# A decode step with a cached attention and a gated layer: w_q loaded first in eight loads of 16 rows, a shorter last stretch, and four tiny loads that nothing reads

## The chip, the cores and the metric

The kernel runs on one core of one Trainium2 chip. Its time is the device time of one execution in microseconds (us). Engines are named as in the profile: PE (TensorE matmul), PEld (its weight loads), DVE (VectorE), ACT (ScalarE), POOL (GpSimd), SP (SyncE, which here only issues loads). A core has 16 DMA engines, which all loads share.

## The reference

One token of 576 numbers goes through a layer norm and then through two branches, whose results are added to the token.

```python
xn  = layernorm(x)                                   # 1 x 576
q   = (xn @ wq) in 32 heads of 128                   # wq: 576 x 4096
k,v = last 4096 rows of the caches, 16 heads, each used by 2 query heads
o   = softmax(q k^T / sqrt(128)) v                   # 32 x 128
a   = o.reshape(4096) @ wo                           # wo: 4096 x 576
z   = gelu(xn @ w_in)                                # w_in: 576 x 4608
b   = (z[:2304] * (w_sp * layernorm(z[2304:]) + b_sp)) @ w_out   # w_out: 2304 x 576
out = x + a + b
```

Everything is bfloat16. Each number of the weights and of the used part of the caches is needed once: w_q 4.72 MB, keys and values 16.78 MB each, w_in 5.31 MB, w_o 4.72 MB and w_out 2.65 MB, 50.96 MB together.

## The kernel before, in words

**Loads.** SP issues all large loads, in the order of the program (L102 to L124): the first quarter of the keys `k0` in two halves, `wq` in two column pieces, `k1`, `v0`, `k2`, `v1`, `k3`, w_in (`win` and a rest `win8`), `v2`, `v3`, w_o (two pieces and a rest `wo28`) and w_out in four pieces: rows 0 to 11, 12 to 15, 16 and 17 of the 18 rows that each partition holds. Each of these loads writes all 128 partitions. The keys and values come in four quarters of four heads, 4.19 MB each.

**Buffers.** Two pools, `small` and `large`, hold two tiles each. A load into a pool's third tile has to wait until the first has been read by its last reader; so `k2` waits for the transposes of `k0`, `v1` for the matmuls with `wq`, and so on. SP issues in order, so a load that waits holds back all that follow.

**Completion counters.** The framework also gives every load, from ACT's three tiny ones on (`x_row` and two of `ws2`), one of eight completion counters in turn. A load first waits until the load that had its counter before has landed. A load that writes over part of what another load writes waits for that one too.

**Compute.** For each quarter b, `turn(b)` (L211) turns the keys with eight DVE transposes, `scores(b)` (L253) multiplies them with the query on PE, with a softmax on DVE and ACT, and `values(b)` (L289) multiplies with the values. The order is written out by hand at L357 to L368, with `turn(0)` at L219 ahead of the query's own work (L222 to L247). Each engine works in this order.

**The end.** `acc` (L378 to L391) sums, in four partition groups, 32 rows of w_o and the first `LATE` = 12 rows of w_out. The two halves of `acc` go to SBUF (`acc_sb`, L392 to L394), `fin` is cleared (L396), and `late` (L398) adds the remaining rows of w_out into `fin`, four matmuls a row. Just ahead of the last row it adds `acc_sb` (L405). `res` copies the result out of `fin` (L409), and SP stores it (L410).

Of the kernel before, what the change touches and what calls it, by code (L numbers as in the profile page):

```python
# [8 lines left out]
FP32 = mybir.dt.float32  # L9
BF16 = mybir.dt.bfloat16  # L10
# [4 lines left out]
P = 128  # L15
D = 576
# [12 lines left out]
NR = 9  # L29
# [3 lines left out]
FR = FH // P  # L33
# [3 lines left out]
ZW = P + ZPAD  # L37
SMALL = NU * DH
LARGE = WR * D
LATE = 12  # L40
OW = D // 4


# [1 line left out]
def kernel(  # L45
# [14 lines left out]
    nc = tc.nc  # L60
    ctx.enter_context(tc.manual_schedule())

    const = ctx.enter_context(tc.tile_pool(name="const", bufs=1))
# [8 lines left out]
    ps_v = ctx.enter_context(tc.tile_pool(name="ps_v", bufs=1, space=PS))  # L72
# [11 lines left out]
    def unit(name, width):  # L84
        pool = small if width == SMALL else large
        return pool.tile([P, width], BF16, name=name, tag="u")

    def halves(a):
        return a.rearrange("k (s c) -> (k s) c", s=2).rearrange("(p r) c -> p (r c)", r=NR)

    def load(t, view, width, cuts):
        for a, e in zip(cuts, cuts[1:]):
            nc.sync.dma_start(t[:, (a - cuts[0]) * width:(e - cuts[0]) * width], view[:, a * width:e * width])

    def load_kv(cache, name, b, width, cuts=(0, NU)):
        t = unit(f"{name}{b}", width)
        src = cache[0, HB * b:HB * (b + 1), SK - W:SK, :].rearrange("s (j u) d -> j s (u d)", u=NU)
        for a, e in zip(cuts, cuts[1:]):
            nc.sync.dma_start(t[:, a * DH:e * DH], src[:, :, a * DH:e * DH])  # L99
        return t  # L100

    kn, vn = {}, {}  # L102
    wq_v, win_v = halves(A_wq), halves(B_w_in)
    wo_v = A_wo.rearrange("(p r) n -> p (r n)", r=WR)
    kn[0] = load_kv(A_k_cache, "k", 0, SMALL, (0, NU // 2, NU))
    wq_t = unit("wq", LARGE)
    load(wq_t, wq_v, 2048, (0, 5, NR))
    kn[1] = load_kv(A_k_cache, "k", 1, SMALL)
    vn[0] = load_kv(A_v_cache, "v", 0, LARGE)
    kn[2] = load_kv(A_k_cache, "k", 2, SMALL)  # L110
    vn[1] = load_kv(A_v_cache, "v", 1, LARGE)
# [9 lines left out]
    wo28 = one.tile([P, FH], BF16, name="wo28", tag="side")  # L121
    load(wo28, wo_v, D, (28, WR))
    wout_t = unit("wout", LARGE)
    load(wout_t, B_w_out.rearrange("(p r) n -> p (r n)", r=FR), D, (0, LATE, 16, 17, FR))  # L124


    ident = const.tile([P, P], BF16, name="ident")
# [83 lines left out]
    def turn(b):  # L211
        for k in range(NK):
            t = ktp.tile([P, 2, 512, 2], BF16, name=f"kt{b}_{k}", tag="kt")
            nc.vector.transpose(  # L214
                t[:].rearrange("p c n e -> p (c n e)").bitcast(FP32),
                kn[b][:, UK * DH * k:UK * DH * (k + 1)].bitcast(FP32).rearrange("p (u c i) -> p c u i", c=2, i=32))
            kt[b, k] = t

    turn(0)  # L219


    q_ps = ps_s.tile([P, 512], FP32, name="q_ps", tag="s")  # L222
# [30 lines left out]
    def scores(b):  # L253
        sm = one.tile([P, 2, 512], FP32, name=f"sm{b}", tag="sm")
        mx = work.tile([P, 2], FP32, name=f"mx{b}", tag="mx")
        for kk in range(2):
            s_ps = ps_s.tile([P, 512], FP32, name=f"s{b}_{kk}", tag="s")
            for k4 in range(4):
                for ce in range(4):
                    c, e = divmod(ce, 2)  # L260
                    nc.tensor.matmul(s_ps[:], lhsT=zq[:, b, ce, ZPAD - 8 * k4:ZPAD - 8 * k4 + P],  # L261
                                     rhs=kt[b, 4 * kk + k4][:, c, :, e],
                                     start=k4 == 0 and ce == 0, stop=k4 == 3 and ce == 3)
            nc.vector.tensor_tensor_reduce(  # L264
                out=sm[:, kk, :].rearrange("p (n s) -> p n s", s=HB),
                in0=s_ps[:].rearrange("p (n s) -> p n s", s=HB),
                in1=cm[:].unsqueeze(1).to_broadcast([P, P, HB]), scale=SCALE, scalar=-3e38,
                op0=ALU.add, op1=ALU.max, accum_out=mx[:, kk:kk + 1])
        m1 = work.tile([P, 1], FP32, name=f"m1{b}", tag="m1")
        nc.vector.tensor_max(m1[:], mx[:, 0:1], mx[:, 1:2])  # L270
        tr = ps_m.tile([P, P], FP32, name=f"tr{b}", tag="m")
        nc.tensor.matmul(tr[:], lhsT=m1[:].to_broadcast([P, P]), rhs=ident_f[:], start=True, stop=True)  # L272
        m8 = work.tile([P, 8], FP32, name=f"m8{b}", tag="m8")
        nc.vector.tensor_reduce(out=m8[:], in_=tr[:].rearrange("p (a x) -> p x a", x=8), axis=AXX, op=ALU.max)
        mj = work.tile([P, 8], FP32, name=f"mj{b}", tag="mj")
        nm = work.tile([P, 1], FP32, name=f"nm{b}", tag="nm")
        nc.vector.tensor_tensor_reduce(out=mj[:], in0=m8[:], in1=sel8[:], scale=-1.0, scalar=0.0,  # L277
                                       op0=ALU.mult, op1=ALU.add, accum_out=nm[:])
        p = one.tile([P, 1024], BF16, name=f"p{b}", tag="p")
        l = work.tile([P, 1], FP32, name=f"l{b}", tag="l")  # L280
        nc.scalar.activation(p[:], sm[:].rearrange("p k n -> p (k n)"), ACT.Exp, bias=nm[:], accum_out=l[:])  # L281
        p_t[b] = work.tile([P, 2, 16, 32], BF16, name=f"pt{b}", tag="pt")
        nc.vector.transpose(p_t[b][:].rearrange("p k u m -> p (k u m)"), p[:])  # L283
        su = ps_m.tile([P, 8], FP32, name=f"su{b}", tag="m")
        nc.tensor.matmul(su[:], lhsT=l[:].to_broadcast([P, P]), rhs=sel8[:], start=True, stop=True)  # L285
        rms[b] = work.tile([P, 8], FP32, name=f"rm{b}", tag="rm")
        nc.vector.reciprocal(rms[b][:], su[:])
# [39 lines left out]
    def gate(z):  # L327
# [26 lines left out]
                                op0=ALU.mult, op1=ALU.add)  # L354
        nc.vector.tensor_mul(hv[:], G[:, 0, :], gz[:])

    scores(0)  # L357
    turn(1)
    scores(1)
# [15 lines left out]
    o_p = const.tile([P, WR], BF16, name="o_p")  # L375
    nc.vector.tensor_copy(o_p[:], op_ps[:])

    acc = [ps_a.tile([P, HW], FP32, name=f"acc{i}", tag="a") for i in range(2)]  # L378
    for i in range(2):
        nc.vector.memset(acc[i][:], 0.0)  # L380
# [4 lines left out]
    rows += [(o_p[:, r:r + 1], wo28[:, D * (r - 28):D * (r - 27)]) for r in range(28, WR)]  # L385
    rows += [(hv[:, r:r + 1], wout_t[:, D * r:D * (r + 1)]) for r in range(LATE)]
    for n in range(0, len(rows), 4):
# [4 lines left out]
    acc_sb = const.tile([P, D], FP32, name="acc_sb")  # L392
    nc.scalar.copy(acc_sb[:, 0:HW], acc[0][:])
    nc.vector.tensor_copy(acc_sb[:, HW:D], acc[1][:])  # L394
    fin = ps_v.tile([P, OW], FP32, name="fin", tag="pv")
    nc.vector.memset(fin[:], 0.0)  # L396

    def late(col, w, n, start=False, stop=False):  # L398
        for g in range(4):
            nc.tensor.matmul(fin[32 * g:32 * g + 1, :], lhsT=col, rhs=w[:, n + OW * g:n + OW * (g + 1)],  # L400
                             start=start, stop=stop, tile_position=(0, 32 * g))

    for r in range(LATE, FR):
        if r == FR - 1:
            late(selu[:, 0:1], acc_sb, 0)  # L405
        late(hv[:, r:r + 1], wout_t, D * r, start=r == LATE, stop=r == FR - 1)

# [33 lines left out]
```

## Time and profile before

| | |
|---|---|
| median of 2 runs | 128.5 us (128.49 to 128.52) |
| the profiled execution | 129.87 us, of which the span from the first to the last instruction is 128.1 us |
| mean granted PE clock | 0.867 |
| busy: PE, DVE, ACT, POOL | 57%, 51%, 8%, 3% of the span |
| DMA | 50.96 MB read, 398 GB/s over the span; SP's queue 93.4% of 16 engines' time |

The span is the profile's time axis, and every position below is counted from its start. The 1.77 us by which the profiled execution is longer than its span lie outside the instructions. The profiled execution was 1.37 us slower than the median of the runs, so a difference is worked out inside the profile and then put on the median.

### The profile page before, as it was taken

Reading aid. Unit: us, or ns where it says so; the run is one execution under the profiler, and the core shown is the slowest. Engines: PE = TensorE matmul, PEld = TensorE weight load, DVE = VectorE, ACT = ScalarE, POOL = GpSimd, SP = SyncE. Lnnn points to the kernel's source line nnn. Section 1 sums busy time; section 2 is a strip of 40 time slices with the busy share of each in tenths; the row PEclk is TensorE's granted clock in tenths of the full one; section 3 lists DMA queues with packets and bytes.
Section 4 is the critical chain, followed back from the end, with each engine's and each line's share of the span. In section 5 each row is a group of like instructions: output and inputs, shape, how many; then the busy total and the mean of one; then the engine's idle time right before and its main releaser. Section 6 shows DMA issues by size and latency. Waiting matters only on the chain.

```text
span 128.1 us, 1363 instructions
## 1 busy us (share of the span) xinstructions
PE 72.9 (57%) x554; PEld 33.7 (26%) x554; DVE 65.3 (51%) x133; ACT 10.2 (8%) x19; POOL 3.9 (3%) x10
## 2 busy tenths in 40 slices
PE   3200007349982399557599554899192389467070
PEld 3100002113421134123234233233080225323040
DVE  6689960060213999640899542998347620300010
ACT  3010000000003000031000031000300030100010
POOL 8400000000000000000000000000000000000000
PEclk9999999999999779986959999589977769855559
DMA  3999999998998999999989998999899899999810
GB/s 82 409 420 444 460 405 414 476 491 348 471 471 368 463 425 389 491 399 420 481 379 450 449 449 368 394 484 460 379 471 435 379 416 438 418 414 436 345 45 0
DMA packets 2899, 51.03 MB, mean 398 GB/s; under 512 B 333, under 2 KB 590, under 8 KB 974
## 3 DMA queue, kind: packets, MB, share of 16 engines
q1 hardware_dynamic: 2888, 50.96, 93.4%
q8 instruction: 4, 0.07, 0.2%
q14 instruction: 1, 0.01, 0.0%
q10 hardware_dynamic: 6, 0.00, 0.0%
HBM read 50.96 MB, written 0.00 MB: 398 GB/s over the span
## 4 chain that ended last, share of the span: by engine, by line
PE 37%; DMA 36%; DVE 16%; ACT 5%; SPq 2%; issue 1%; ACTq 0%
PE s L261 22%; DMA wout<-in_B_w_out_dram 19%; DMA wq<-in_A_wq_dram 17%; DVE kt L214 9%; PE pv L295 4%; ACT p L281 4%; PE z L319 3%; DVE sm L264 2%; PE op L303 2%; PE tr L272 2%; PE q_ps L225 2%; PE acc L390 1%; PE fin L400 1%; DVE pt L283 1%; SPq L99 1%
## 5 line engine op out<-in xcount | busy, mean ns | idle before, releaser
L261 PE MATMUL s<-kt,zq 128*128 128x512 bf16 x128 | 36.4, 448 | 5.3 <-DVE kt L214 4.9
L214 DVE STREAM_TRANSPOSE kt<-k 128x1024 f32<-128x1024 f32 x32 | 36.4, 1205 | 0.0
L261 PEld LDWEIGHTS <-zq 128*128 128x128 bf16 x128 | 14.0, 110 | 26.5 <-issue 15.3
L225 PE MATMUL q_ps<-wq,xw 128*32 128x512 bf16 x36 | 4.2, 626 | 16.4 <-DMA wq<-in_A_wq_dram 16.4
L264 DVE CUSTOM_DVE_ANT_1 sm<-s,cm 128x512 f32<-128x512 f32 x8 | 5.4, 677 | 10.1 <-PE s L261 10.1
L281 ACT ACTIVATE p<-sm,nm 128x1024 bf16<-128x1024 f32 x4 | 4.6, 1147 | 73.9 <-DVE nm L277 73.9
L295 PE MATMUL pv<-v,pt 128*32 128x512 bf16 x128 | 10.2, 477 | 0.0
L283 DVE STREAM_TRANSPOSE pt<-p 128x1024 bf16<-128x1024 bf16 x4 | 5.0, 1245 | 5.4 <-ACT p L281 5.4
L306 DVE TENSOR_TENSOR o_t<-op,rm 128x8 bf16<-128x8 f32 x4 | 0.7, 167 | 13.0 <-PE op L303 13.0
L225 PEld LDWEIGHTS <-xw 128*32 128x32 bf16 x36 | 1.4, 131 | 18.4 <-issue 18.4
L394 DVE COPY acc_sb<-acc 128x288 f32<-128x288 f32 x1 | 0.5, 458 | 11.2 <-PE acc L390 11.2
L285 PE MATMUL su<-sel,l 128*128 128x8 f32 x8 | 1.6, 266 | 7.6 <-ACT p L281 7.6
L303 PE MATMUL op<-selu,pvs 128*128 128x8 f32 x32 | 4.2, 259 | 2.8 <-ACT pvs L300 2.8
L390 PE MATMUL acc<-wo,o_p 128*1 128x288 bf16 x64 | 4.4, 439 | 1.7 <-DMA wo<-in_A_wo_dram 1.7
L303 PEld LDWEIGHTS op<-selu,pvs 128*128 128x128 f32 x32 | 3.9, 191 | 5.1 <-ACT pvs L300 5.1
L229 DVE CAST q_sb<-q_ps 128x512 bf16<-128x512 f32 x1 | 0.7, 692 | 8.2 <-PE q_ps L225 8.2
L295 PEld LDWEIGHTS <-pt 128*32 128x32 bf16 x128 | 3.6, 114 | 4.3 <-issue 2.6
L272 PE MATMUL tr<-ident_f,m 128*128 128x128 f32 x8 | 2.0, 326 | 3.9 <-DVE m L270 3.9
L319 PE MATMUL z<-win,xw 128*32 128x288 bf16 x72 | 3.6, 376 | 0.0
L285 PEld LDWEIGHTS su<-sel,l 128*128 128x128 f32 x8 | 1.2, 187 | 8.4 <-ACT p L281 8.4
L390 PE MATMUL acc<-wout,hv 128*1 128x288 bf16 x24 | 1.6, 438 | 3.0 <-DMA wout<-in_B_w_out_dram 3.0
L300 ACT COPY pvs<-pv 128x512 f32<-128x512 f32 x4 | 2.3, 586 | 11.0 <-PE pv L295 11.0
(95 smaller groups left out, 43.4 us busy)
## 6 DMA issues: line engine op xcount, KB each, us to landing
v<-in_A_v_cache_dram SPq DMA_DIRECT2D x4, 4096.0 KB, 25.8
k<-in_A_k_cache_dram SPq DMA_DIRECT2D x3, 4096.0 KB, 36.7
win<-in_B_w_in_dram SPq DMA_DIRECT2D x1, 4608.0 KB, 25.7
k<-in_A_k_cache_dram SPq DMA_DIRECT2D x2, 2048.0 KB, 9.8
wo<-in_A_wo_dram SPq DMA_DIRECT2D x2, 2016.0 KB, 27.1
wq<-in_A_wq_dram SPq DMA_DIRECT2D x1, 2560.0 KB, 17.4
wq<-in_A_wq_dram SPq DMA_DIRECT2D x1, 2048.0 KB, 21.6
wout<-in_B_w_out_dram SPq DMA_DIRECT2D x1, 1728.0 KB
```

What stands on the lines that cost most here:

```text
L214: nc.vector.transpose(t[:].rearrange("p c n e -> p (c n e)").bitcast(FP32), kn[b][:, UK * DH * k:UK * DH * (k + 1)].bitcast(FP32).rearrang ...
L225: nc.tensor.matmul(q_ps[32 * g:32 * g + 32, :], lhsT=xw[:, r, :], rhs=wq_t[:, 2048 * r + 512 * g:2048 * r + 512 * (g + 1)], start=r == 0, ...
L261: nc.tensor.matmul(s_ps[:], lhsT=zq[:, b, ce, ZPAD - 8 * k4:ZPAD - 8 * k4 + P], rhs=kt[b, 4 * kk + k4][:, c, :, e], start=k4 == 0 and ce = ...
L264: nc.vector.tensor_tensor_reduce(out=sm[:, kk, :].rearrange("p (n s) -> p n s", s=HB), in0=s_ps[:].rearrange("p (n s) -> p n s", s=HB), in ...
L272: nc.tensor.matmul(tr[:], lhsT=m1[:].to_broadcast([P, P]), rhs=ident_f[:], start=True, stop=True)
L281: nc.scalar.activation(p[:], sm[:].rearrange("p k n -> p (k n)"), ACT.Exp, bias=nm[:], accum_out=l[:])
L283: nc.vector.transpose(p_t[b][:].rearrange("p k u m -> p (k u m)"), p[:])
L285: nc.tensor.matmul(su[:], lhsT=l[:].to_broadcast([P, P]), rhs=sel8[:], start=True, stop=True)
L295: nc.tensor.matmul(pv[32 * g:32 * g + 32, :].rearrange("p (n d) -> p n d", n=4), lhsT=p_t[b][:, kk, u, :], rhs=v4[:, kk, u, :, :], start=k ...
L303: nc.tensor.matmul(op[:], lhsT=pvs[:, DH * u:DH * (u + 1)], rhs=selu[:, 8 * u:8 * u + 8], start=u == 0, stop=u == 3)
L319: nc.tensor.matmul(zp[i][32 * g:32 * g + 32, :], lhsT=xw[:, r, :], rhs=rhs, start=r == 0, stop=r == NR - 1, tile_position=(0, 32 * g))
L390: nc.tensor.matmul(acc[i][32 * g:32 * g + 1, :], lhsT=col, rhs=w[:, HW * i:HW * (i + 1)], start=n == 0 and g > 0, stop=n + 4 >= len(rows), ...
```

## The change

There are five edits.

- `wq` is loaded ahead of `k0`, in eight loads of 16 rows in place of two loads of 128 rows. Load e writes the partitions e, e+8, e+16, ... e+120, each with its whole row of 36,864 bytes.
- Behind `k1` come four loads into a new tile `few`: 8, 4, 2 and 1 rows of 64, 80, 96 and 112 bytes. They are cut from w_o, and nothing reads `few`. All four write its first row, so they overlap.
- `turn(0)` moves from ahead of the query's work to the line before `scores(0)`.
- `LATE` goes from 12 to 8, and w_out comes in five pieces: rows 0 to 7, 8 to 12, 13 to 15, 16 and 17.
- `fin` is made and cleared ahead of `acc`, and `acc_sb` is added ahead of row 13 instead of row 17.

```diff
-LATE = 12
+LATE = 8
...
+    wq_t = unit("wq", LARGE)
+    for e in range(8):
+        nc.sync.dma_start(wq_t[e::8, :], wq_v.rearrange("(i e) f -> e i f", e=8)[e])
     kn[0] = load_kv(A_k_cache, "k", 0, SMALL, (0, NU // 2, NU))
-    wq_t = unit("wq", LARGE)
-    load(wq_t, wq_v, 2048, (0, 5, NR))
     kn[1] = load_kv(A_k_cache, "k", 1, SMALL)
+    few = const.tile([16, 64], BF16, name="few")
+    for n, k in enumerate((8, 4, 2, 1)):
+        nc.sync.dma_start(few[0:k, 0:32 + 8 * n], A_wo[0:k, 0:32 + 8 * n])
     vn[0] = load_kv(A_v_cache, "v", 0, LARGE)
...
-    load(wout_t, B_w_out.rearrange("(p r) n -> p (r n)", r=FR), D, (0, LATE, 16, 17, FR))
+    load(wout_t, B_w_out.rearrange("(p r) n -> p (r n)", r=FR), D, (0, LATE, 13, 16, 17, FR))
...
-
-    turn(0)
...
+    turn(0)
     scores(0)
...
+    fin = ps_v.tile([P, OW], FP32, name="fin", tag="pv")
+    nc.vector.memset(fin[:], 0.0)
     acc = [ps_a.tile([P, HW], FP32, name=f"acc{i}", tag="a") for i in range(2)]
...
-    fin = ps_v.tile([P, OW], FP32, name="fin", tag="pv")
-    nc.vector.memset(fin[:], 0.0)
...
     for r in range(LATE, FR):
-        if r == FR - 1:
+        if r == 13:
             late(selu[:, 0:1], acc_sb, 0)
         late(hv[:, r:r + 1], wout_t, D * r, start=r == LATE, stop=r == FR - 1)
```

## The prediction

> **What bounds the kernel now.** I read the page's DMA row, then busy time by stage, then the chain that ended last, then SP's own timeline. The page's DMA row (40 slices, tenths of 16 engines) and one stage of 120 us:
>
> ```profile
> DMA  3999999998998999999989998999899899999810
> 2.00:122.00 120.00, 70.48 (x510) 32.48 (x514) 63.39 (x127) 9.80 (x18) 2.53 (x3) 0.87 1.00 424
> ```
>
> From 2 to 122 us the DMA engines are busy all the time (share 1.00), at 424 GB/s, while PE works 70 and DVE 63 of the 120 us. So the kernel is one stream of 50.96 MB; what matters is when it starts, whether it pauses, and what comes after its last byte. The chain, from the issue of w_out on:
>
> ```profile
> 97.30 24.18 DMA wout<-in_B_w_out_dram
> ...
> 121.52 1.64 PE acc L390 x24
> ...
> 123.19 0.46 DVE acc_sb L394
> ...
> 123.67 0.19 DVE fin L396
> ...
> 123.90 1.33 PE fin L400 x26
> ...
> 125.26 0.31 DVE res L409
> ```
>
> W_out is issued at 97.3 and waits 24 us behind other loads: the compute is far ahead of the stream. Behind it stand 3.7 us of work, and the store. SP's timeline (start, length of the issue):
>
> ```profile
> 0.74 1.29 SPq L99 DMA_DIRECT2D k<-in_A_k_cache_dram  x2
> 2.06 1.20 SPq L93 DMA_DIRECT2D wq<-in_A_wq_dram  x2
> 3.30 0.54 SPq L99 DMA_DIRECT2D k<-in_A_k_cache_dram  x1
> 3.89 0.60 SPq L99 DMA_DIRECT2D v<-in_A_v_cache_dram  x1
> 18.17 0.53 SPq L99 DMA_DIRECT2D k<-in_A_k_cache_dram  x1
> ```
>
> `v0` is issued at 3.9, while in the trace's DMA packet records its first packet starts at 33.1, when `k1`'s last ones end (33.1 to 33.6 by engine). That queue of 29 us is what lets SP wait without cost.
>
> **The tiny loads: a pause in the stream.** The instruction list of the changed kernel gives SP's waits (DMAHW are the eight counters):
>
> ```
> few<-in_A_wo_dram 8x32 [waits DMAHW6]
> few<-in_A_wo_dram 4x40 [waits DMAHW7,DMAHW6]
> few<-in_A_wo_dram 2x48 [waits DMAHW7,DMAHW0]
> few<-in_A_wo_dram 1x56 [waits DMAHW1,DMAHW0]
> v_112<-in_A_v_cache_dram 128x1x16384 [waits DMAHW2]
> ```
>
> Counting the loads off in turn, the first of the two in the second to fourth lines (in one of them the second) is an eighth of w_q, and the other is the tiny load just before. So each tiny load is issued only when the one before has landed, and `v0`, `k2`, `v1` and all else wait behind them on SP. The 8-row load stands behind `k1` in the same queue. In the packet records a load's packets follow those of the load issued before, engine by engine, so it lands when `k1` has left its engines. Then nothing large is queued, and the DMA engines run dry. Two rows price a small load:
>
> ```profile
> 0.73 0.50 ACTq L77 DMA_DIRECT2D x_row<-in_A_x_dram  x1
> 2.02 1.19 PE L161 MATMUL x_ps<-one_bf,x_row 1*64 1x1 bf16 x9 [2.02 <-DMA x_row<-in_A_x_dram]
> ```
>
> `x_row` is issued at 0.73 and PE uses it at 2.02: 1.29 us from issue to use, with nothing ahead of it. The result's store gives nearly the same: issued at 125.59, its packets run at 126.85 to 126.93. A large load that starts a stream takes 1.42 us from issue (0.74) to first packet (2.16, packet records). From a load's last packet to its reader it is 0.5 us (w_q: 23.94 to PE at 24.42; w_out's first piece: 120.96 to 121.52).
>
> The bytes ahead of the tiny loads are as before (k0, w_q, k1), so `k1` leaves at 33.1 to 33.6, mean 33.35. The 8-row load has landed for SP at 33.6 + 0.5 = 34.1. The 4-row load lands at 35.4, the 2-row load at 36.7. The 1-row load is issued then (0.54, as other issues of SP), and nobody waits for it soon. `v0` is issued at 37.2, first packet 38.6. The pause is 38.6 − 33.35 = **5.25 us**. Bounds: 0.90 us from issue to first packet (x_row's, in the records) plus 0.1 for the landing makes 1.0 for each of the two waited loads and for `v0`'s start: 34.1 + 2.0 + 0.25 (the issue) + 1.0, less 33.35 = 4.0 us; the 0.25 is near the shortest issue on ACT, 0.21. Above, each of the two may wait out half as much again (1.29 to 2.0, since the rows it stands on are one load from an idle queue): 6.7.
>
> [...]
>
> A stream that starts is slow at first: of `k0`'s first 16 packets eight took 1.16 to 1.69 us and eight about 0.73, against 0.611 later; `k0`'s first half ended about 0.9 us later than eight packets at 0.611 would. I add **0.9** for the second start (nothing to 0.9).
>
> **w_q first, in eight loads.** The bytes are the same. 36,864-byte packets run at the same rate as others (w_in: 1.368 us each, 26.9 GB/s an engine; k0: 16,384 in 0.611, 26.8), so 8 packets an engine take 10.95 us, as the two pieces now. SP's issues cost 8 × 0.6 in place of 2, each covers 1.37 us of packets, so the engines don't starve. The sixth to eighth loads wait for ACT's `x_row` and the two loads of `ws2`. In the records the words of `ws2` take turns with SP's packets, one at a time: first at 3.97, last completion at 6.42, four packets later. With 1.37 us packets from 2.2 on that is 9.6 + 0.5; the eighth load's first packet comes 1.3 us later, 11.4, and seven packets plus the slow start last until 12.7. Hidden, with 1.3 us to spare; if not, the stream pauses by what is missing, and `k0`, `k1` queue behind that wait. The first load has 16 rows in place of 128: its first packet may come in 1.26 us (the store's) in place of 1.42: I take **−0.2** (−0.5 by x_row's 0.90, nothing at the other end).
>
> **turn(0) later.** `k0`'s halves now land at 19.4 and 24.3, as w_q's 11 us stand ahead. q's work (4.3 us of matmuls from 14.4 on, then 2.0 on DVE and PE) ends at 20.7, `turn(0)` at 30.3. `turn(1)` follows `scores(0)`'s end (4.8 us of softmax, as in the chain at 37.8 to 42.4) and runs 36 to 45.6. That releases `k3`, which the stream wants at 38.6 + 3 × 9.76 (4.19 MB at 0.43) = 67.9. Likewise: w_in issued at 55, wanted 77.6; v2 68, 90; v3 80, 99.7; w_o 88, 109.5; w_out 101, 121. The last piece of w_out also waits for `v3`'s landing (112, wanted 128). At least 15 us remain everywhere, so these moves cost nothing; if this cover were gone, each late issue would be a pause of its lateness.
>
> **The shorter end.** From the last w_out packet (123.13) plus 0.5 the last row can be used at 123.65; now `res` starts at 125.26, since `acc` with 12 rows, the copies, the clearing and 28 matmuls of `fin` come first. Counted back on the slowest engine: rows 0 to 7 usable at 120.0; 16 matmuls of `acc` 1.1 to 121.1; copies 0.46 to 121.6; rows 8 to 12 land at 121.7, 20 matmuls 0.77; `acc_sb`'s 0.68 to 123.2; rows 13 to 15 at 0.15 a row to 123.65; rows 16 and 17 to 124.0. So `res` starts at 124.05: **−1.2** (none to −1.6, the last landing). The new packet sizes cost 0.05 an engine by the rates of w_out's present pieces.
>
> **Sum:** +5.25 + 0.9 − 0.2 − 1.2 = +4.75. On the profiled execution 129.87 + 4.75 = 134.6; the median runs were 1.37 lower, so **133.2**. Its own range, from the bounds: 128.5 + 4.0 − 0.5 − 1.6 = 130.4 up to 128.5 + 6.7 + 0.9 = 136.1.
>
> **Rivals.**
>
> *Half the destinations.* Each of the eight loads writes one partition in eight, where every load in this trace writes all 128. No row shows what that costs: if what limits an engine to 26.9 GB/s is the side it writes to and engines share it, w_q's 10.95 us become 21.9: +10.95, **144.2**; if engines that share take turns and drift apart, half of that, 138.7. Against: the engines' rate is the same for rows of 4,608 to 36,864 bytes (25.3 to 27.0 GB/s in the records), as a limit of each engine's own would make it. That does not exclude it, since in these loads all destinations are in use. What decides is whether w_q's packets take 1.37 or 2.7 us. The pause then only starts 11 us later.
>
> [...]
>
> *Not slower: the tiny loads pass.* If the tiny loads don't queue behind `k1`, their chain runs from about 12 us on beside the stream, `v0` is issued long before 33, and the gains are left: 128.5 − 1.4 = **127.1**. It decides if the 2-row load lands before about 31.3 (33.35 less v0's 1.42 and an issue). For it: `ws2`'s words came through between k0's packets. Against: they were on ACT's queue; on SP's the records show no load before its turn. That the change doesn't do what it says would come out here too; the waits in the list speak against it.
>
> *A short pause.* Each step at its lower bound, with no slow second start: 130.4 to 131.0, within 2%.
>
> **How the numbers follow.** Two per cent, about what a measurement of this kernel can tell from no change, is 125.9 to 131.1. Forecast 0.52 (131.1 to 136.1); half destinations 0.30 (0.23 in full, 0.07 halfway); short pause 0.09; tiny loads pass 0.06; 0.03 for an early end better than bounded. Range 130.5 to 145: it leaves out the passing loads, the early end and part of the short pause, about 0.15. Faster 0.02, same 0.14, slower 0.84.
>
> **What would show it.** The DMA row of the new page should have a slice near 33 to 38 us with little or nothing in it, and SP three issues some 1.3 us apart there; w_q's packets should stay at 1.37 us, and its reader start near 14.4 (near 25 if half the destinations count). After the pause the DMA share should be 1.00 to the end, and the last piece of w_out be followed by `res` within 1 us. Wrong it would be if w_q is slow, if `v0` is issued before `k1` lands, or if a later load is issued after the stream wanted it.

## The result, and the profile after

The changed kernel takes **146.4 us** (146.15 and 146.57) against 128.5 us before: 1.136 times as long, with a 95% interval of 1.130 to 1.143. The forecast was 133.2 us and its range ended at 145. The sign was right, the size was not.

The page of the changed kernel, its rows for DMA share and rate in GB/s (40 slices of 3.6 us), and SP's queue:

```profile
DMA  7899899999993289999999999989999998999950
GB/s 164 174 255 225 163 194 192 390 427 440 427 436 152 73 363 436 436 436 436 436 436 436 436 436 448 470 358 406 502 436 431 418 436 374 429 429 403 401 202 0
...
q1 hardware_dynamic: 3030, 50.96, 91.3%
```

The two rows have to be read together. By its share the DMA is busy in the first seven slices, but it moves 163 to 255 GB/s there, half of the 424 that the stream moved before. Then come five slices at the full rate, a hole of two (152 and 73 GB/s, shares 3 and 2 tenths), and from there the stream runs as before. By stage (the windows view; columns: window, its length, busy time of PE, PEld, DVE, ACT, POOL, granted clock, DMA share, GB/s):

```profile
2.00:26.00 24.00, 1.95 (x12) 1.71 (x12) 5.29 (x21) 1.76 (x3) 2.53 (x3) 1.00 1.00 214
26.00:44.00 18.00, 13.85 (x73) 5.39 (x73) 11.71 (x17) 0.00 (x0) 0.00 (x0) 1.00 1.03 441
44.00:50.00 6.00, 1.06 (x5) 0.71 (x6) 4.01 (x10) 1.24 (x2) 0.00 (x0) 0.93 0.20 53
50.00:139.00 89.00, 55.13 (x425) 24.99 (x423) 43.11 (x82) 7.19 (x14) 0.00 (x0) 0.77 0.99 422
```

A packet counts whole in the window in which it starts, so a share can come out a little above 1.00. The first row is w_q and the third is the pause. SP's timeline has the pause's cause (start, length with the waits inside the group):

```profile
0.73 7.12 SPq L107 DMA_DIRECT2D wq<-in_A_wq_dram  x8
7.90 5.14 SPq L99 DMA_DIRECT2D k<-in_A_k_cache_dram  x3
15.15 33.38 SPq L112 DMA_DIRECT2D few<-in_A_wo_dram  x4
48.58 0.55 SPq L99 DMA_DIRECT2D v<-in_A_v_cache_dram  x1
```

The four tiny loads hold SP from 15.2 to 48.5 us, and `v0` is issued at 48.6, 3.3 us after `k1`'s last packet (45.3 in the packet records). The end of the chain:

```profile
123.44 17.46 DMA wout<-in_B_w_out_dram
140.90 0.04 issue
140.94 0.32 PE fin L403 x4
141.26 0.02 issue
141.28 0.31 DVE res L412
```

After the last piece of w_out only the last four matmuls and the copy are left.

The DMA packet records place the 16.3 us between the two spans (128.1 and 144.4). On the mean of the 16 engines `k1` ends at 33.4 before and 44.9 after: +11.5 for w_q. From there to `v0`'s first packet it is 0.0 before and 5.4 after. From `v0`'s first packet to w_out's last it is 89.6 and 89.9: +0.3. The latest packet to `res` is 2.1 and 0.8: −1.3; `res` to the span's end +0.3. The sum is +16.2; the missing 0.1 is that the latest of the last packets comes 0.25 us after their mean, where it came 0.16 after it before.

### The profile page after: what moved, and what is told of

Same layout as the page of the kernel before. It is cut to its first block, busy times and chain, and to the rows that moved or that the text cites. A ratio compares the mean times of both kernels' runs of the same rounds, so it can differ in the third digit from the quotient of the medians.

```text
span 144.4 us, 1392 instructions
## 1 busy us (share of the span) xinstructions
PE 74.0 (51%) x562; PEld 34.2 (24%) x562; DVE 65.4 (45%) x133; ACT 10.2 (7%) x19; POOL 3.9 (3%) x10
## 4 chain that ended last, share of the span: by engine, by line
DMA 70%; PE 19%; DVE 7%; ACT 2%; issue 1%; SPq 0%; ACTq 0%
DMA v<-in_A_v_cache_dram 25%; DMA wq<-in_A_wq_dram 17%; DMA k<-in_A_k_cache_dram 15%; PE s L263 13%; DMA wout<-in_B_w_out_dram 12%; PE q_ps L227 3%; DVE kt L218 2%; ACT p L283 2%; PE pv L297 1%; DVE sm L266 1%; DVE pt L285 1%; PE tr L274 1%; DVE zq L240 1%; DVE q_sb L231 0%; DVE m L276 0%
## 5 line engine op out<-in xcount | busy, mean ns | idle before, releaser
L263 PE MATMUL s<-kt,zq 128*128 128x512 bf16 x128 | 37.0, 455 | 12.9 <-DVE kt L218 12.8
L297 PE MATMUL pv<-v,pt 128*32 128x512 bf16 x128 | 12.2, 551 | 3.9 <-DMA v<-in_A_v_cache_dram 3.9
L395 PE MATMUL acc<-wo,o_p 128*1 128x288 bf16 x64 | 3.6, 382 | 0.7 <-DMA wo<-in_A_wo_dram 0.7
L350 PE MATMUL sz_ps<-sz,ones_f 128*128 128x2 f32 x2 | 0.6, 364 | 4.5 <-DVE sz L347 4.5
```

What stands on the lines that cost most here:

```text
L297: nc.tensor.matmul(pv[32 * g:32 * g + 32, :].rearrange("p (n d) -> p n d", n=4), lhsT=p_t[b][:, kk, u, :], rhs=v4[:, kk, u, :, :], start=k ...
L395: nc.tensor.matmul(acc[i][32 * g:32 * g + 1, :], lhsT=col, rhs=w[:, HW * i:HW * (i + 1)], start=n == 0 and g > 0, stop=n + 4 >= len(rows), ...
```

## The experiments

**One load for w_q.** The eight loads are replaced by one of 128 rows, with all else as in the changed kernel.

```diff
-    for e in range(8):
-        nc.sync.dma_start(wq_t[e::8, :], wq_v.rearrange("(i e) f -> e i f", e=8)[e])
+    load(wq_t, wq_v, 2048, (0, NR))
```

> The changed kernel, with w_q first in one load of 128 rows in place of the eight of 16. Theory (the eight loads each write only one partition in eight, and engines share what they write to): w_q's packets of 36,864 bytes go from 2.89 us back to 1.37 us, the first reader of w_q starts 11.5 us earlier, and the time falls by 11.5 us to about 134.9. Rival (w_q is slow because it stands first, at the start of the stream): the packets stay near 2.9 us and the time near 146.

It took 134.6 us (134.2 to 134.8), 1.045 times the kernel before (1.039 to 1.050). W_q's packets are back at 1.364 us, and the page's row of rates (slices of 3.3 us) has lost the slow start and kept the hole:

```profile
GB/s 178 388 499 365 419 448 444 434 453 316 8 158 473 414 375 473 473 375 414 473 473 375 414 506 355 532 295 524 375 424 468 453 359 432 417 406 431 395 137 0
```

So the eight loads cost 11.8 us, and that w_q stands first costs nothing of the kind. This is also the kernel that the forecast had described, and its 134.6 lies inside the range of the forecast alone (130.4 to 136.1).

**Without the tiny loads.** The eight loads stay.

```diff
-    few = const.tile([16, 64], BF16, name="few")
-    for n, k in enumerate((8, 4, 2, 1)):
-        nc.sync.dma_start(few[0:k, 0:32 + 8 * n], A_wo[0:k, 0:32 + 8 * n])
```

> The changed kernel without the four tiny loads. Theory (the chain of waits empties the stream for 5.4 us on the mean of the engines, and the stream starts again slowly): the pause between the packets of k1 and v0 goes, the time falls by 5.4 to 5.8 us to 140.6 to 141.0. Rival (the late issue of what follows matters, or the tiny loads were hidden): it stays over 143.

It took 140.2 us (140.05 to 140.31): the tiny loads cost 6.2 us, 0.4 more than the most that was expected. In the packet records `k1` ends at 44.80 on the mean and `v0` begins at 44.80. W_q's packets still take 2.87 us.

**Both taken out.**

> The changed kernel with one load of 128 rows for w_q and without the tiny loads: what is left is w_q ahead of k0, turn(0) later and the shorter end. Theory: the end alone counts, 1.0 to 1.3 us less than before, 127.2 to 127.5. Rival (w_q first or the late turn(0) costs something too): 128.5 or more.

It took 128.16 us against 128.61, a ratio of 0.9958 (0.9935 to 0.9981). What is left of the change brings about 0.5 us, less than half of what was expected; the interval stays below 1, so this version is slightly faster than both kernels. Each of the two costs is nearly the same with and without the other: 6.2 and 6.4 us for the tiny loads, 11.8 and 12.0 for the eight loads.

**Tiny loads without overlap.** One load for w_q, and each tiny load into columns of its own.

```diff
-    few = const.tile([16, 64], BF16, name="few")
+    few = const.tile([16, 256], BF16, name="few")
...
-        nc.sync.dma_start(few[0:k, 0:32 + 8 * n], A_wo[0:k, 0:32 + 8 * n])
+        nc.sync.dma_start(few[0:k, 64 * n:64 * n + 32 + 8 * n], A_wo[0:k, 0:32 + 8 * n])
```

> As the run with one load for w_q (134.6 us) and with the four tiny loads, but each into columns of its own, so that none writes over another. Theory (the chain of waits is the pause): without the overlap SP issues all four and v0 long before k1 has landed, no pause between k1 and v0, and the time is that of the run without tiny loads and with one load for w_q, 128.2 us. Rival (tiny loads of few rows, or a load on fewer than 16 engines, hold up the stream as such): 131 us or more, with a pause behind k1.

It took 128.5 us, 0.9975 times the kernel before (0.9947 to 1.0003), 6 us less than with the overlap. SP's timeline of this kernel:

```profile
3.33 11.53 SPq L111 DMA_DIRECT2D few<-in_A_wo_dram  x4
14.90 0.54 SPq L99 DMA_DIRECT2D v<-in_A_v_cache_dram  x1
```

The same four loads now leave SP at 14.9 us, and `v0` is queued 18 us before it is needed. So the loads themselves cost little (128.51 us against 128.16 without them, in two series of runs); the waits that their overlap causes are the pause.

**The cost of 16-row loads by itself.** In this kernel and the next two of its kind everything is left out but loads of parts of w_q and a copy of x to the output. Each group has eight loads of about 18,400 bytes a row, and each group has a packet size of its own, so that the records tell them apart.

```python
def step8(n):       # every eighth partition, source rows eight apart
    nc.sync.dma_start(big[n::8, cols(n, 8)], apart[n][:, 0:C - 8])
def step8_near(n):  # every eighth partition, 16 neighbouring source rows
    nc.sync.dma_start(big[n::8, cols(n, 16)], src[16 * n:16 * n + 16, 0:C - 16])
# step7, step4 (within one half), step1 (16 neighbours), then all 128 rows
```

> Only loads, of parts of w_q, and x copied to the output; everything else of the computation is left out. Six groups of eight loads, each of 16 rows of about 18,400 bytes (0.69 us a packet at the rate of all loads of before) but the last group of 128 rows. They differ in the partitions that are written: every eighth (as in the changed kernel), every eighth from 16 neighbouring source rows, every seventh, every fourth of one half, 16 neighbours; last all 128. [...] Rival one (the source addresses, 16 rows far apart): every eighth from neighbouring rows 0.69, all others with far rows 1.44, 16 neighbours too. Rival two (loads of one packet an engine are slow as such): all five groups 1.44, the last 0.69.

The median packets were 1.41 us for every eighth partition with far source rows, 1.42 with near ones, 1.12 for every seventh, 1.43 for every fourth, 2.28 for 16 neighbours, and 0.686 for all 128. So near and far source rows gave the same time, and with the same far rows it goes from 1.12 to 2.28 us with the partitions written: they count. But no 16-row group ran at 0.69 us, so this run doesn't exclude that such loads are slow for a second reason too. Two values, 1.12 and 2.28 us, are no whole multiples of 0.686 (1.6 and 3.3 times). Here each load's partitions differ from those of the load before; whether that makes these values was not tested by itself. So the next run keeps the partitions of a group fixed. It also reads the same source rows in all eight loads of a group, which this one did not.

**The same with fixed partitions.**

```python
def group(g, rows, step):
    last = (rows - 1) * step + 1
    for n in range(8):
        nc.sync.dma_start(big[0:last:step, C * n:C * n + C - 8 * g], src[0:rows, 0:C - 8 * g])
```

> Only loads, of parts of w_q, and x copied to the output; everything else of the computation is left out. Ten groups of eight loads, packets of about 18,400 bytes (0.69 us at full rate), each group always on the same partitions, so that loads that overlap in time write to the same places. Sixteen rows on partitions with step 8, 7, 4, 1; then eight rows (eight engines) with step 4, 8, 12, 16, 2, 1. [...] Rival (the number of rows or engines of a load decides): 1.4 for all of the first four and one value for all of the last six. Rival (eight neighbouring partitions are one place): step 8 0.69, step 4 1.4, step 1 5.5; then 1.4, 0.69, 0.69, 0.69, 2.75, 5.5.

| rows, step | median packet, us | in units of 0.684 us |
|---|---|---|
| 16, 8 | 1.438 | 2.10 |
| 16, 7 | 1.385 | 2.02 |
| 16, 4 | 1.438 | 2.10 |
| 16, 1 | 2.699 | 3.95 |
| 8, 4 | 0.684 | 1.00 |
| 8, 8 | 1.433 | 2.10 |
| 8, 12 | 0.682 | 1.00 |
| 8, 16 | 1.431 | 2.09 |
| 8, 2 | 1.425 | 2.08 |
| 8, 1 | 2.690 | 3.93 |

Three values come out: 0.68, 1.4 and 2.7 us, so one, about two and about four times the shortest. Engines that slow each other in this way are said here to write to one place; that they do is read from the packet times alone.

The windows view of this kernel shows four of the groups (16 rows with step 8 and 1; 8 rows with step 4 and 8; columns: window, length, POOL's busy time, clock, DMA share, GB/s):

```profile
3.00:13.50 10.50, 0.00 (x0) 1.00 1.05 216
...
38.00:56.00 18.00, 0.00 (x0) 1.00 0.98 105
58.00:63.00 5.00, 0.00 (x0) 1.00 0.49 206
65.00:73.50 8.50, 0.00 (x0) 1.00 0.51 104
```

A share of 1.05 with 216 GB/s is the picture of w_q in the changed kernel (1.00 with 214); eight rows with step 4 (share 0.49, 206 GB/s) move nearly as much as 16 with step 8. If four engines write to one place in the group of 16 neighbours, where a packet of 18,368 bytes takes 2.699 us, a place takes 4 × 18,368 / 2.699 us = 27.2 GB/s by this estimate, about one engine's rate in the group of 8 rows with step 4 (18,352 bytes in 0.684 us, 26.8). The six groups of 8 rows are the cleanest evidence: they read the same rows and differ, but for a few bytes of packet size, only in the partitions written, and take 0.68, 1.43 and 2.69 us. So the number of rows or engines does not decide. The places of eight neighbouring partitions do not fit either (8 rows with step 8 and 4 would change roles; they took 1.433 and 0.684 us). For which other partitions this holds, these groups do not show.

**Where some engines share and others don't.**

> Only loads, of parts of w_q, and x copied to the output; everything else of the computation is left out. Eight groups of eight loads, always on the same partitions within a group: 16 rows with step 7; 8 rows with step 7, 5 and 9; 16 rows with step 5; 4 rows with step 35, 4 and 1. [...]

Engines are told apart here by following the packets in time. With 8 rows and step 7 two engines took 1.35 us a packet and the other six 0.685, side by side. With 4 rows and step 35 it was 1.35 for two of four; with 4 rows and step 1 2.7 us. So in these groups a load does not move at its slowest engine's pace: some engines ran at half the rate beside others at the full one. The 16-row groups again had one value for all engines: step 7 1.40, step 5 1.43. The groups of 8 rows with step 5 and 9 and of 4 rows with step 4 ran beside packets of their neighbour groups; they give no single value (medians 0.73, 0.78 and 0.80 us) and decide nothing.

**Four loads of 32 rows.**

```diff
-    for e in range(8):
-        nc.sync.dma_start(wq_t[e::8, :], wq_v.rearrange("(i e) f -> e i f", e=8)[e])
+    for e in range(4):
+        nc.sync.dma_start(wq_t[e::4, :], wq_v.rearrange("(i e) f -> e i f", e=4)[e])
```

> The changed kernel (146.4 us) with w_q in four loads of 32 rows (every fourth partition) in place of eight of 16 (every eighth). [...]

It took 134.5 us (one run), the time of one load. The page's row of rates:

```profile
GB/s 178 356 500 389 390 425 444 479 464 326 8 158 464 375 425 474 454 365 444 474 444 365 454 496 367 478 332 505 385 454 449 405 405 413 433 408 426 398 168 0
```

The half rate at the start is gone, and only the hole of the tiny loads is left (8 and 158 GB/s). The packets of w_q take 1.364 us once the stream has started. So w_q can be cut into several loads at no cost. These loads differ from those of 16 rows in two things, the partitions they write (every fourth, not every eighth) and the number of rows (32, not 16), and no run separates these two for loads on all 16 engines.

**The shorter end alone, on the kernel before.**

```diff
-LATE = 12
+LATE = 8
...
-    load(wout_t, B_w_out.rearrange("(p r) n -> p (r n)", r=FR), D, (0, LATE, 16, 17, FR))
+    load(wout_t, B_w_out.rearrange("(p r) n -> p (r n)", r=FR), D, (0, LATE, 13, 16, 17, FR))
... fin cleared ahead of acc, acc_sb added ahead of row 13, as in the change
```

> The kernel before with the shorter end alone: LATE 8, w_out in five pieces, fin cleared early, acc_sb added ahead of row 13. Theory (the end is all that the good part of the change brings): 128.1 to 128.3, as with w_q first in one load. Rival (w_q first gives it, by its earlier first packet): 128.5 to 128.7, nothing gained; or it takes something away, and this run is 127.7 or less.

The ratio is 0.9973 with an interval of 0.9945 to 1.0002: 0.35 us less, and nothing at all is not excluded (the medians are 128.61 and 128.65). It does not tell the two theories apart. Its profile, of an execution of 129.54 us, shows what else can set the end:

```profile
119.60 3.40 PE L392 MATMUL acc<-wo,o_p 128*1 128x288 bf16 x64
124.83 0.31 DVE L409 CAST res<-fin 97x144 bf16<-97x144 f32 x1 [0.82 <-PE fin L400]
```

The matmuls with w_o run from 119.6 to 123.0, although the last packet of w_out's first piece ended at 119.6, and `res` starts 1.6 us after w_out's last packet (123.20). Here the compute, and not the stream, came last, so little of the time was left for a shorter end to save. In the two profiles of the kernel before, these matmuls were done at 118.5 and 120.3, ahead of that piece (121.0 and 120.8).

**The kernel before, profiled again.**

> The kernel before, unchanged, for a second profile of it: the first profiled execution was 1.4 us over the median of its runs, and the comparison of the ends hangs on it. If the 1.4 us stood in the stream or at its end, this profile's stretch from the last w_out packet to the copy of the result shows by how much the end can get shorter (2.1 us in the first profile, 0.8 us in the changed kernel).

This execution took 128.47 us with a span of 126.7. Its end, in the windows view, first in the profile that the prediction stood on and then in the second:

```profile
121.00:126.00 5.00, 2.90 (x56) 1.48 (x55) 0.94 (x3) 0.40 (x1) 0.00 (x0) 0.60 0.17 63
```

```profile
121.00:125.00 4.00, 1.70 (x56) 1.02 (x55) 0.94 (x3) 0.40 (x1) 0.00 (x0) 1.00 0.19 67
```

The same 56 matmuls take 2.90 us of PE time at a granted clock of 0.60, and 1.70 at 1.00. From w_out's last packet to `res` it is 0.9 us in the second profile (122.96 to 123.85), not the 2.1 of the first. In such an execution that leaves little for a shorter end to gain.

## Why the prediction was wrong, point by point

**w_q in eight loads: the step that failed.** "The bytes are the same. 36,864-byte packets run at the same rate as others", and so w_q's cost was put at nothing. The packets took 2.87 to 2.89 us, not 1.37. The eight loads cost 11.8 to 12.0 us, two thirds of the whole difference. The row it stood on, w_in's, was of a load to all 128 partitions, and so was every row that was brought as evidence against the rival (one rate for all row sizes). None of them could speak on loads to one partition in eight. The rival *half the destinations* had the mechanism, and its 10.95 us were 7 to 9% too low: the packets took 2.1 times as long (2.88 us for 1.37; in the groups of 8 rows 1.43 for 0.68), not twice. It was given 0.30 and should have weighed more, as no row spoke against it. That shared places slow a load by this factor is shown by the groups of 8 rows; whether loads of 16 rows are also slow for a second reason stays open.

**The top of the range.** It was the rival's 144.2 and under 1 us more, without the rival's own spread; the sum's own top of 136.1 and the rival's 10.95 make 147.1. With the measured costs put in the rival comes to 128.5 + 11.9 + 6.3 − 0.5 = 146.2, against 146.4 measured. These costs are differences from the same kernel, so that agreement is no test of its own.

**The tiny loads: right in the mechanism, and in the sum partly by luck.** Forecast was a pause of 5.25 us and 0.9 for the second start, 6.15 together; the runs give 6.2 (with the eight loads) and 6.4 (without). The parts were off: between `k1` and `v0` the engines stood for 5.4 and 5.9 us on the mean, and from `v0`'s first packet to w_out's last the stream took only 0.3 and 0.2 us longer than without the tiny loads, where 0.9 was put down for the second start. In the records of the changed kernel the tiny loads' packets stand at 45.0, 46.6, 47.9 and 49.1 and `v0`'s first at 49.9, so a step of the chain took 1.6, 1.3 and 1.3 us, where 1.29 was taken. The cause, a chain of waits made by the overlap, is shown by the run with the tiny loads apart. The top of the pause, 6.7 us, has two steps of 2.0 us, an estimate of the author's (half as much again as `x_row`'s 1.29); here the steps were 1.3 to 1.6 (2.0 once, in the run with one load).

**The shorter end: too large, and even its sign is not sure.** Forecast 1.2 us. The whole rest of the change, with w_q first, brings 0.5 us (0.2 to 0.8 by its interval), and the shorter end alone 0.35 (none to 0.7). The term was worked out on an execution whose PE clock was 0.60 at the end, in which a 3.7 us tail stood behind the stream. And "the compute is far ahead of the stream" was read from the issue of w_out; the matmuls with w_o were done only 0.5 us ahead of w_out's first piece in the second profile and 3.4 us behind it in the profile of the shorter end. The warning was in the numbers: that execution was 1.37 us slower than the median of the runs.

**The earlier first packet: too large for 16 rows.** Forecast −0.2; w_q's first packet came at 2.14, against 2.16 for `k0` before. As one load of 128 rows it came at 1.75, and `k1` ended 0.4 to 0.5 us earlier; why the larger load starts sooner was not tested.

**turn(0) later and the other waits: no cost seen.** They were put at nothing. With both costs taken out the time is 0.5 us below the kernel before, so a cost of theirs could only hide behind a gain of the same size; and after the pause the stream ran at a share of 0.99.

## What to carry to other kernels

In a kernel that is one stream of loads, ask of each load which partitions it writes, and not only how many bytes and rows it has: here 16 rows with a step of 8 halved the rate (214 GB/s while w_q was loaded), 32 rows with a step of 4 did not (410), and the DMA share was 1.00 in both. Read the rate beside the share. A load that writes over part of an earlier one waited for it here, so that rows of 64 to 112 bytes held SP's queue until 48.5 us and cost 6.2 to 6.4 us, and with columns of their own next to nothing (128.51 us against 128.16); give such loads columns of their own. And before a gain is taken from the last microseconds of one profile, see whether that execution is a usual one.

## What the runs showed that was not expected

- Sixteen rows with step 7 or 5 ran at 1.39 to 1.43 us a packet on every engine; of eight rows with step 7, two engines took 1.35 us and six 0.685. These groups read the same 16 or 8 rows in every load, and in no run did a group of 16-row loads take less than 1.12 us a packet. Why all engines are slow in the 16-row case stays open, and so does whether the same slowed w_q's loads too.
- A first load of 128 rows sent its first packet at 1.75 us, one of 16 rows only at 2.14.
- The granted PE clock in the last 5 us was 0.60 in one execution of the kernel before and 1.00 in another. PE's work there took 2.90 and 1.70 us, which accounts for most of the 1.4 us between their times.
